# Token-wise attention product in one run, two heads on the two halves of the array's rows; FFN units on three PSUM banks

## The chip, the cores and the metric

One core of one Trainium2 chip. The time is what the device takes for one execution, in microseconds, as a median of several executions. The kernel before takes 315.76 us (315.75 to 315.96 in 3 runs). Engines are named as in the profile: PE (TensorE), PEld (its weight loads), DVE, ACT, POOL, and SP, which here only issues DMAs.

## The reference, cut to what matters

```python
kv  = einsum('bhsd,bhse->bhde', k, v)        # 8 batches, 8 heads, 576 tokens, 64 per head
out = einsum('bhsd,bhde->bhse', q, kv)
rms = sqrt(mean(out * out, axis=-1, keepdims=True) + 1e-6)
x   = (out / rms * g_norm)                   # laid out as (8 * 576 tokens, 512)
y   = ((x @ w_a) * (x @ w_b)) @ w_out        # d_ff = 1536
```

The FFN is the bulk of the work. It runs in 9 strips of 512 tokens. The attention of batch s+1 is worked on during strip s, between the FFN's matmuls. A batch has 576 tokens and a strip 512, so a strip needs only the first part of the newest batch.

## The kernel before

A strip has 12 units (eight matmuls of 512 columns each: `a`, then `b`) and 4 output pieces (12 matmuls each). A slot number `n` counts them, `n + 0.5` is the middle of the next one. For batches 2 to 7, x is made by token: `tx` multiplies a chunk of 128 tokens by the kv matrices of two heads at once, which stand as two 64x64 blocks on the diagonal of a 128x128 matrix `kvb` with zeros elsewhere. The squares, sums and scaling follow on ACT, DVE and POOL, and a transposing DMA on the SP queue brings the chunk into `xt`, from which the FFN's matmuls read.

```python
def tx(self, c, i):                                  # chunk c into bank i
    for p in range(NP):                              # 4 pairs of heads
        nc.tensor.matmul(P[:, i, p * 128 : (p + 1) * 128],
            lhsT=self.qT[:, p, t0 : t0 + 128], rhs=kvb[self.b % 2][:, p, :], start=True, stop=True)
    nc.scalar.activation(sqt[c % 3][r], self.by_head(i)[r], AF.Square)
# tss: DVE sum; trs: ACT reciprocal root, POOL scale; then
def txt(self, c, i):
    nc.vector.tensor_mul(t[r], self.by_head(i)[r], sqt[c % 3][r])
    nc.sync.dma_start_transpose(xt[:, :, ...], ...)  # x transpose, on the SP queue
...
AB = (4, 1, 2, 0)                                    # PSUM banks of the FFN units, in turn
...
if s == 1: k0, xs = 5, (6.5, 8, 9.5, 11, 12.5)       # slots: kv product, chunks 0..4
...                                                  # txt of a chunk: 2.5 slots after its tx
for s in range(1, N_STRIP - 1):
    for n in range(FC + 4):
        ...  ffn_ab or ffn_o (its output store goes to the SP queue), then slot(A, s, n)
        if b + 1 < B and n == (12, 4, 8, 5, 8)[s - 1]:
            transpose_q(b + 1)                       # q load, transposing, on the SP queue
        if b + 2 < B and n == (14, 10, 14, 8)[s - 1]:
            load_late(b + 2)                         # q, k, v of batch b+2, issued by POOL
```

X transposes, output stores and q loads share one queue, and their order on it is the order in which this program issues them.

## Time and profile before

| | before |
|---|---|
| time, median | 315.76 us |
| PE busy | 98% of the span |
| matmul of the FFN, 512 columns | issues every 216 ns |
| token-wise product | 120 matmuls, 56 ns each, 6.7 us |

From the page of the kernel before, the busy shares and the chain that ended last:

```profile
span 313.9 us, 4977 instructions
PE 308.9 (98%) x1907; PEld 147.9 (47%) x1907; DVE 141.6 (45%) x235; ACT 115.9 (37%) x225; POOL 101.2 (32%) x123
...
PE 98%; ACT 1%; issue 0%; DVE 0%
```

PE is the bound: its work makes up 98% of the chain. The longest wait of PE, in the waits view (engine, line, waited for: us in total, times, longest), is one of the start:

```profile
PE P L400 <- DVE eps_t L417: 1.2, 1, 1.2
```

The timeline of PE gives the costs (start, length, engine, source line, instruction, shapes, count). The ends of matmuls are modelled and overlap, so costs are read from starts. First the token-wise product of one chunk, between units:

```profile
64.22 0.39 PE L265 MATMUL P<-kvb,qT 128*128 128x128 bf16 x4
64.44 1.03 PE L315 MATMUL P<-xt,wb_t 128*128 128x512 bf16 x4
```

Four matmuls of the product (L265) move the next group from 64.22 to 64.44 us: 0.22 us, 56 ns each. Then a kv burst, which runs in pairs on the two halves of the array's columns:

```profile
124.29 1.03 PE L315 MATMUL P<-xt,wb_t 128*128 128x512 bf16 x4
125.25 1.46 PE L168 MATMUL P<-vtl,ktl 128*64 128x64 bf16 x80
126.63 1.04 PE L315 MATMUL P<-xt,wa_t 128*128 128x512 bf16 x4
127.51 1.03 PE L315 MATMUL P<-xt,wb_t 128*128 128x512 bf16 x4
```

With 0.863 us for a group of four FFN matmuls, the burst of 80 moves what follows by 127.51 - 0.863 - (124.29 + 0.863) = 1.49 us. The bursts of 40 move it by 0.86 us. So a pair takes about 31.7 ns and a burst about 0.23 us besides.

### The profile page before, as it was taken

How to read it: one execution, taken by the hardware profiler on the slowest of the kernel's cores; microseconds unless marked ns; L12 is line 12 of the kernel's file. 1: busy time of each engine (PE TensorE's matmuls, PEld its weight loads, DVE VectorE, ACT ScalarE, POOL GpSimd, SP SyncE). 2: the span in 40 equal slices, each digit the busy share in tenths (PEclk: the TensorE clock that was granted, in tenths of full speed). 3: DMA queues.
4: the chain of work that ended last, by engine and by line, in shares of the span. 5: the costliest groups of instructions: out<-in, count | busy, mean ns of one | idle time of the engine just before them, and what ended most of it. 6: DMA issues, size and time to landing. Idle time of an engine off the chain costs nothing.

```text
span 313.9 us, 4977 instructions
## 1 busy us (share of the span) xinstructions
PE 308.9 (98%) x1907; PEld 147.9 (47%) x1907; DVE 141.6 (45%) x235; ACT 115.9 (37%) x225; POOL 101.2 (32%) x123
## 2 busy tenths in 40 slices
PE   8999999999999999999999999999999999999995
PEld 3544454444445444544454445544544444444443
DVE  4544335456337703583377123761683134214321
ACT  3643255453246313451364024622651233123310
POOL 8954990282453730148138200320230000000000
PEclk9999999999999999999999999999999999999999
DMA  8999999999899999059999980073022200030002
GB/s 181 196 196 199 201 186 166 230 136 152 165 162 184 103 199 151 2 58 162 212 120 130 158 186 2 19 159 109 3 50 60 102 0 0 33 102 1 0 34 101
DMA packets 94253, 36.19 MB, mean 115 GB/s; under 512 B 64918, under 2 KB 89750, under 8 KB 94230
## 3 DMA queue, kind: packets, MB, share of 16 engines
q0 software_dynamic: 59120, 18.44, 54.3%
q1 hardware_dynamic: 34642, 16.87, 24.7%
q10 hardware_dynamic: 468, 0.57, 0.6%
q8 instruction: 15, 0.25, 0.3%
q14 instruction: 8, 0.07, 0.1%
HBM read 37.78 MB, written 12.98 MB: 162 GB/s over the span
## 4 chain that ended last, share of the span: by engine, by line
PE 98%; ACT 1%; issue 0%; DVE 0%
PE P L315 60%; PE P L372 30%; PE P L265 2%; PE P L400 2%; PE P L168 2%; PE P L192 1%; PE P L219 1%; PE P L206 0%; ACT sq L215 0%; PE P L245 0%; PE P L458 0%; ACT o_end L610 0%; PE P L462 0%; PE P L474 0%; DVE zeros L411 0%
## 5 line engine op out<-in xcount | busy, mean ns | idle before, releaser
L333 DVE TENSOR_TENSOR ab<-P,asb 128x512 bf16<-128x512 f32 x108 | 74.5, 691 | 103.6 <-PE P L315 86.0
L315 PE MATMUL P<-xt,wa_t 128*128 128x512 bf16 x432 | 111.9, 380 | 0.0
L315 PE MATMUL P<-xt,wb_t 128*128 128x512 bf16 x432 | 111.7, 379 | 0.0
L329 ACT CAST asb<-P 128x512 bf16<-128x512 f32 x108 | 63.0, 585 | 92.7 <-PE P L315 92.7
L372 PE MATMUL P<-wo_t,ab 128*128 128x512 bf16 (+1 forms) x444 | 95.8, 374 | 0.0
L372 PEld LDWEIGHTS <-ab 128*128 128x128 bf16 x444 | 43.0, 98 | 48.6
L315 PEld LDWEIGHTS <-wa_t 128*128 128x128 bf16 x432 | 41.4, 98 | 47.4 <-issue 0.2
L315 PEld LDWEIGHTS <-wb_t 128*128 128x128 bf16 x432 | 41.5, 98 | 46.9
L288 POOL TENSOR_TENSOR sqt<-rst,g_all 128x512 f32<-128x512 f32 (+1 forms) x24 | 25.0, 1043 | 96.2 <-ACT rst L281 96.2
L385 ACT COPY osb<-P 128x512 f32<-128x512 f32 x17 | 9.9, 585 | 67.3 <-PE P L372 57.5
L387 DVE COPY osb<-P 128x512 f32<-128x512 f32 x18 | 12.4, 691 | 44.1 <-PE P L372 39.5
L139 POOL DMA_DIRECT2D qs<-in_q_dram x12 | 19.8, 1653 | 0.7 <-issue 0.3
L276 DVE TENSOR_REDUCE sst<-sqt 128x8 f32<-128x512 f32 (+1 forms) x24 | 16.3, 680 | 1.8 <-ACT sqt L272 1.1
L297 DVE TENSOR_TENSOR qv<-P,sqt 128x512 bf16<-128x512 f32 (+1 forms) x24 | 16.4, 685 | 0.3
L272 ACT ACTIVATE sqt<-P 128x512 f32<-128x512 f32 (+1 forms) x24 | 14.4, 599 | 4.2 <-PE P L265 4.1
L265 PEld LDWEIGHTS <-qT 128*128 128x128 bf16 x120 | 9.2, 98 | 7.1
L265 PE MATMUL P<-kvb,qT 128*128 128x128 bf16 x120 | 11.6, 219 | 0.0
L281 ACT ACTIVATE rst<-sst,eps_t 128x8 f32<-128x8 f32 (+1 forms) x30 | 9.0, 300 | 4.6 <-DVE sst L276 4.3
L233 DVE SCALAR_TENSOR_TENSOR xt<-P,g_col,rs 128x288 bf16<-128x288 f32 x16 | 7.5, 512 | 5.2 <-ACT rs L223 5.2
L288 POOL TENSOR_TENSOR k_x<-rst,g_all 128x512 f32<-128x512 f32 x6 | 6.3, 1042 | 8.8 <-ACT rst L281 8.8
L131 POOL DMA_DIRECT2D wo_t<-in_moe_w_out_dram x12 | 6.4, 530 | 6.7 <-DMA wb_t<-in_moe_w_b_dram 3.2
L400 PE MATMUL P<-zeros 128*128 128x512 bf16 x17 | 7.2, 568 | 1.2 <-DVE eps_t L417 1.2
(67 smaller groups left out, 119.4 us busy)
## 6 DMA issues: line engine op xcount, KB each, us to landing
out_dram<-osb SPq DMA_DIRECT2D x23, 256.0 KB, 2.1
qs<-in_q_dram POOLq DMA_DIRECT2D x12, 288.0 KB, 7.0
ktl<-in_k_dram POOLq DMA_DIRECT2D x6, 512.0 KB, 9.2
vtl<-in_v_dram POOLq DMA_DIRECT2D x6, 512.0 KB, 11.9
out_dram<-osb SPq DMA_DIRECT2D x13, 128.0 KB, 2.4
wo_t<-in_moe_w_out_dram POOLq DMA_DIRECT2D x12, 128.0 KB, 6.0
wa_t<-in_moe_w_a_dram POOLq DMA_DIRECT2D x5, 256.0 KB, 9.0
wb_t<-in_moe_w_b_dram POOLq DMA_DIRECT2D x5, 256.0 KB, 9.6
```

The source lines that it names most:

```text
L139: nc.gpsimd.dma_start(out=d[:, hs, :], in_=q[b, hs].rearrange("h t d -> t h d"))
L265: nc.tensor.matmul(P[:, i, p * 128 : (p + 1) * 128], lhsT=self.qT[:, p, t0 : t0 + 128], rhs=kvb[self.b % 2][:, p, :], start=True, stop=True,)
L272: nc.scalar.activation(sqt[c % 3][r], self.by_head(i)[r], AF.Square)
L276: nc.vector.reduce_sum(sst[c % 3][r], sqt[c % 3][r], axis=mybir.AxisListType.X)
L288: nc.gpsimd.tensor_mul(sqt[c % 3][r], rst[c % 3][r].unsqueeze(2).to_broadcast([n, H, D]), g_all[r].unsqueeze(1).to_broadcast([n, H, D]),)
L297: nc.vector.tensor_mul(t[r], self.by_head(i)[r], sqt[c % 3][r])
L315: nc.tensor.matmul(self.a if w is wa_t else self.b, lhsT=w[:, kc, self.fc * 128 : (self.fc + 1) * 128], rhs=xt[:, kc, t0 : t0 + STRIP], st ...
L329: nc.scalar.copy(self.t, self.a)
L333: nc.vector.tensor_mul(abt[self.s % 2][self.fc], self.b, self.t)
L372: nc.tensor.matmul(P[:, i, e0:e1], lhsT=abt[s % 2][fc][:, g * 128 : (g + 1) * 128], rhs=wo_t[:, fc, e0:e1], start=(fc == 0), stop=(fc == F ...
L387: nc.vector.tensor_copy(t, P[:, i, :])
L400: nc.tensor.matmul(P[:, i, 0:cols], lhsT=zeros[:, 0:128], rhs=zeros[:, 0:cols], start=True, stop=True)
```

## The change

Its intent: with the zero blocks gone, two heads can use the upper and the lower 64 rows of the array at the same time, 64 columns each. A change of the array's mode costs something (about 0.2 us a run, as read below), so all of chunks 0 to 3 of a batch are computed in one run, into banks 4 to 7 (the two heads of a pair in different banks). The last, half-used chunk (LC) stays 128 rows wide and goes into bank 3. It is now handled first, so that bank 3 is free for the output pieces. The units are left with banks 0 to 2.

```diff
-        def tx(self, c, i):
+        def tx(self):
             for p in range(NP):
                 nc.tensor.matmul(
-                    P[:, i, p * 128 : (p + 1) * 128],
-                    lhsT=self.qT[:, p, t0 : t0 + 128],
+                    P[:, O, p * 128 : (p + 1) * 128],
+                    lhsT=self.qT[:, p, S - 128 : S],
                     rhs=kvb[self.b % 2][:, p, :],
...
+            for c in range(LC):
+                for p in range(NP):
+                    for j, (i, c0) in enumerate(self.place(c)):   # banks 4..7
+                        r = slice(j * D, (j + 1) * D)
+                        nc.tensor.matmul(
+                            P[:, i, c0 + p * D : c0 + (p + 1) * D],
+                            lhsT=self.qT[r, p, t0 : t0 + 128],
+                            rhs=self.kvs[r, p, :],
...
-    AB = (4, 1, 2, 0)
+    ab_banks = [4, 1, 2, 0]            # later [0, 1, 2]
...
+        k0, x0 = {1: (5, 6.5), 2: (2, 3.5), 3: (5, 6.5), 4: (0, 1.5), 5: (5, 6.5), 6: (0, 1.5)}[s]
...
-                a.kv_out(slice(0, NP), kb[:, i], nc.vector.tensor_copy if i else nc.scalar.copy)
+                nc.vector.tensor_copy(a.kvs, kb[:, i])
+                a.kv_out(slice(0, NP), kb[:, i])
+        if n == x0:
+            A.tx()
+        for i, c in enumerate((LC, *range(LC))):
+            m = n - x0                 # tsq at 1.5 * i; tss at (1, 2, 4, 5, 7)[i];
+            ...                        # trs half a slot, txt 1.5 slots after tss
...
-            if b + 2 < B and n == (14, 10, 14, 8)[s - 1]:
+            if b + 2 < B and n == (14, 11, 14, 9)[s - 1]:
                 load_late(b + 2)
```

More of the change, by code (lines that the diff above doesn't have):

```diff
@@ L78 @@
     k32 = k_x[0:EP].rearrange("p (h c d) -> p h c d", h=2, c=EC)
-    sqt = [sb([128, H, D], FP32, f"sqt{i}") for i in range(2)]
-    sqt.append(k_x[:, 0 : H * D].rearrange("p (h d) -> p h d", h=H))
+    sqt = [sb([128, 2, NP, D], FP32, f"sqt{i}") for i in range(2)]
+    sqt.append(k_x[:, 0 : H * D].rearrange("p (j h d) -> p j h d", j=2, h=NP))
     sst = [sb([128, H], FP32, f"sst{i}") for i in range(3)]
@@ L257, in rows, with place, by_head @@
             return t0, slice(c * 128 - t0, 128)
-        def by_head(self, i):
-            return P[:, i, :].rearrange("t (h d) -> t h d", h=H)
-        def tx(self, c, i):
-            t0, r = self.rows(c)
+        def place(self, c):
+            return tuple((4 + 2 * j + c // 2, c % 2 * (STRIP // 2)) for j in range(2))
+        def by_head(self, c):
+            if c == LC:
+                return P[:, O, :].rearrange("t (p j d) -> t j p d", j=2, p=NP)
+            (i, c0), (j, _) = self.place(c)
+            o = P[:, i : j + 1 : j - i, c0 : c0 + STRIP // 2]
+            return o.rearrange("t j (p d) -> t j p d", p=NP)
+        def tx(self):
             for p in range(NP):
                 nc.tensor.matmul(
-                    P[:, i, p * 128 : (p + 1) * 128],
-                    lhsT=self.qT[:, p, t0 : t0 + 128],
+                    P[:, O, p * 128 : (p + 1) * 128],
+                    lhsT=self.qT[:, p, S - 128 : S],
                     rhs=kvb[self.b % 2][:, p, :],
@@ L271, in tx, with tsq @@
                 )
-            nc.scalar.activation(sqt[c % 3][r], self.by_head(i)[r], AF.Square)
+            for c in range(LC):
+                t0, _ = self.rows(c)
+                for p in range(NP):
[5 more added lines that the diff above has]
+                            rhs=self.kvs[r, p, :],
+                            start=True,
+                            stop=True,
+                        )
+        def tsq(self, c):
+            _, r = self.rows(c)
+            nc.scalar.activation(sqt[(c + 1) % (LC + 1) % 3][r], self.by_head(c)[r], AF.Square)
         def tss(self, c):
             _, r = self.rows(c)
-            nc.vector.reduce_sum(sst[c % 3][r], sqt[c % 3][r], axis=mybir.AxisListType.X)
+            nc.vector.reduce_sum(
+                sst[(c + 1) % (LC + 1) % 3][r],
+                sqt[(c + 1) % (LC + 1) % 3][r].rearrange("t j p d -> t (j p) d"),
+                axis=mybir.AxisListType.X,
+            )
         def trs(self, c):
@@ L281, in trs @@
             nc.scalar.activation(
-                rst[c % 3][r],
-                sst[c % 3][r],
+                rst[(c + 1) % (LC + 1) % 3][r],
+                sst[(c + 1) % (LC + 1) % 3][r],
                 AF.Abs_reciprocal_sqrt,
@@ L288, in trs, with txt @@
             nc.gpsimd.tensor_mul(
-                sqt[c % 3][r],
-                rst[c % 3][r].unsqueeze(2).to_broadcast([n, H, D]),
+                sqt[(c + 1) % (LC + 1) % 3][r].rearrange("t j p d -> t (j p) d"),
+                rst[(c + 1) % (LC + 1) % 3][r].unsqueeze(2).to_broadcast([n, H, D]),
                 g_all[r].unsqueeze(1).to_broadcast([n, H, D]),
             )
-        def txt(self, c, i):
+        def txt(self, c):
             t0, r = self.rows(c)
             t = x_tok[c // 3][:, c % 3]
-            nc.vector.tensor_mul(t[r], self.by_head(i)[r], sqt[c % 3][r])
+            nc.vector.tensor_mul(
+                t[r].rearrange("t (p j) d -> t j p d", j=2), self.by_head(c)[r], sqt[(c + 1) % (LC + 1) % 3][r]
+            )
             t0 += self.b * S
@@ L337, in rest @@
             self.part_b(kcs)
-    AB = (4, 1, 2, 0)
-    n_ab = [0]
+    ab_banks = [4, 1, 2, 0]
     def ab_bank():
-        n_ab[0] += 1
-        return AB[(n_ab[0] - 1) % len(AB)]
+        ab_banks.append(ab_banks.pop(0))
+        return ab_banks[-1]
     def ffn_ab(s, fc, between=None):
@@ L516 @@
     u3.part_b()
-    n_ab[0] = 0
     for fc in range(4, FC):
@@ L550 @@
     u1.rest((3,))
-    n_ab[0] = 1
+    ab_banks[:] = [0, 1, 2]
     def slot(A, s, n):
@@ L568, in slot @@
             for i, a in enumerate(two):
-                a.kv_out(slice(0, NP), kb[:, i], nc.vector.tensor_copy if i else nc.scalar.copy)
-        for c, x in enumerate(xs):
-            i = 5 + c % 3
-            if n == x:
-                A.tx(c, i)
-            elif n == x + 0.5:
+                nc.vector.tensor_copy(a.kvs, kb[:, i])
[4 more added lines that the diff above has]
+            m = n - x0
+            if m == 1.5 * i:
+                A.tsq(c)
+            if m == (1, 2, 4, 5, 7)[i]:
                 A.tss(c)
-            elif n == x + 1:
+            if m == (1, 2, 4, 5, 7)[i] + 0.5:
                 A.trs(c)
-            elif n == x + 2.5:
-                A.txt(c, i)
+            if m == (1, 2, 4, 5, 7)[i] + 1.5:
+                A.txt(c)
     for s in range(1, N_STRIP - 1):
```

## The prediction

> **What bounds the kernel.** TensorE. The page gives PE 98% busy at full granted clock; the chain that ended last is 98% PE and after the start holds no wait worth naming. DVE (45%), ACT (37%), POOL (32%) have room. So only PE's issue time counts, unless PE is made to wait. In the timeline an FFN matmul of 512 columns issues every 216 ns (12 in 2.59 us), a unit of eight takes 1.73 us.
>
> **What changes on PE.** For batches 2 to 7 the token-wise attention product is 20 matmuls of 128x128 (120 in all). The timeline shows four of them moving the next group by 0.22 us: 56 ns each, weight loads hidden; six batches cost 6.7 us. Afterwards the last, half-used chunk stays so (4 matmuls). The 16 others become 32 of 64 rows by 64 columns, in pairs on the two halves of the array's rows, without the zero blocks.
>
> What a pair costs is not in the trace. The nearest thing is the k·v product: pairs on two halves of the *columns*, 64 columns each. A burst of 40 moves the next group by 0.86 us, one of 80 by 1.49 us: 31.7 ns a pair, plus 0.23 us fixed per burst. The Trainium skill says both: "TensorE: Matmul & The Clock Gate", Part 3, that row tiles run concurrently; "TensorEngine Tiling (Array Packing)", Key Properties, that a change of tiling mode drains the array. The trace agrees for column halves; no run shows yet that 64-row by 128-column weight loads keep that pace.
>
> Estimate per batch: before 16 x 56 = 0.89 us; after 16 x 31.7 ns + 0.23 us = 0.73 us. Gain 0.16 us, times six 1.0 us, all of it on the critical path. One run per batch keeps the fixed cost below the gain.
>
> **What changes elsewhere.** Squares, reductions, scalings stay the same in number and size, spread over 8.5 units rather than 7.5. The kv copies add one DVE copy (about 0.4 us) per batch; all half-block copies (about 0.37 us) now go to ACT, four in a row (1.5 us) where two batches are prepared; the product needs them 2.6 us after the kv burst. Not critical.
>
> Three banks instead of four for the units: a bank is written again 1.73 us after its group's issue ends. From the timeline the ACT eviction is done 0.78 us, the DVE multiply 0.97 us after that end: slack 0.95 and 0.76 us. Two 0.68 us DVE jobs between two multiplies fit with about 0.3 us delay, less than the slack. I expect no or only tenths of a microsecond of PE waits.
>
> **Prediction.** 314.8 us (0.3% faster), 8 in 10 between 314.1 and 316.4. Faster by over 2%: 0.01; within 2%: 0.96; slower by over 2%: 0.03.
>
> **What would show it.** Right: the 32 narrow matmuls plus 4 wide ones move the following group by about 0.95 us a batch, against 1.12 us for the 20 before; no idle before FFN matmuls. Three-bank step wrong: FFN matmuls waiting on the asb copy or ab multiply. Pair step wrong: the run takes 1.1 to 1.4 us.
>
> **What would make it wrong.** If the halves run one after another, 32 x 29 ns plus the fixed cost is 1.16 us a batch: 1.6 us slower in all. If weight loads of 64 rows don't hide (no pace under 53 ns a pair), about 1 us slower. If DVE's order makes a multiply wait over 0.8 us for a reduction, each batch could lose 0.5 us. A larger drain for row halves also eats the gain.

## More of the kernel before

Last the SP queue near the end of strip 1.

```profile
76.39 1.11 SPq L365 DMA_DIRECT2D out_dram<-osb  x2
77.60 1.25 SPq L299 DMA_TRANSPOSE xt<-qv  x1
79.02 2.63 SPq L151 DMA_TRANSPOSE qT<-qs  x1
81.75 0.99 SPq L365 DMA_DIRECT2D out_dram<-osb  x2
82.83 1.90 SPq L299 DMA_TRANSPOSE xt<-qv  x1
```

The x transpose at 77.60 us is that of chunk 2, the last one that strip 2 needs. The trace has no time of landing for it (the moment at which a DMA's data are in place), but strip 2 started at 83.47 us without a wait, so it had landed by then. The q load behind it holds SP for 2.63 us.

## The result, and the profile after

The changed kernel takes 320.25 us (319.04 to 320.56 in 5 runs), the kernel before in the same rounds 315.76 us: ratio 1.0135, 95% interval 1.0117 to 1.0154. A ratio is the mean time of one kernel's runs over that of the other's of the same rounds, so not quite the ratio of the medians quoted. Executions over 1.5% slower than the fastest of the same kernel are left out of the means. I had predicted 314.8 us, with a range up to 316.4.

The page of the changed kernel, with the parts shown of before:

```profile
span 318.5 us, 5155 instructions
PE 309.3 (97%) x2003; PEld 146.0 (46%) x2003; DVE 142.3 (45%) x237; ACT 117.5 (37%) x229; POOL 101.0 (32%) x123
...
PE 84%; DMA 8%; POOL 4%; issue 1%; DVE 0%; SPq 0%; ACT 0%; POOLq 0%; DVEq 0%
```

DMAs are now in the chain that ended last. The waits view for PE names them:

```profile
PE P L346 <- DMA xt<-qv: 2.6, 1, 2.6
PE P L430 <- DVE eps_t L447: 1.2, 1, 1.2
PE P L168 <- DMA vtl<-in_v_dram: 1.2, 1, 1.2
```

The middle one is the start of the kernel and stood before, too. There is no FFN matmul (L346, L402) that waits for ACT or DVE: the three banks cost nothing. The two others are new.

The run itself went better than predicted (timeline of PE):

```profile
64.26 0.39 PE L275 MATMUL P<-kvb,qT 128*128 128x128 bf16 x4
64.58 0.64 PE L287 MATMUL P<-kvs,qT 64*128 64x64 bf16 x32
65.15 1.04 PE L346 MATMUL P<-xt,wb_t 128*128 128x512 bf16 x4
66.03 1.03 PE L346 MATMUL P<-xt,wa_t 128*128 128x512 bf16 x4
```

It moves what follows by 66.03 - 0.863 - 64.26 = 0.91 us, where the 20 matmuls of before moved it by 5 x 0.22 = 1.12 us: 0.21 us gained per batch, 1.3 us for six. The starts of the single matmuls in the trace show where the time goes: the two of a pair start 3 to 4 ns apart, and a pair follows every 29 ns. The first narrow matmul starts 0.15 us after the last wide one, and the next FFN matmul 0.12 us after the last narrow one. In `e4_full_rows` below, where the mode does not change, these distances are 0.06 and 0.03 us. So the two changes of mode cost about 0.09 us each.

**First wait, at the start of strip 2.** The SP queue:

```profile
76.44 1.11 SPq L395 DMA_DIRECT2D out_dram<-osb  x2
77.65 1.25 SPq L330 DMA_TRANSPOSE xt<-qv  x1
79.07 2.35 SPq L151 DMA_TRANSPOSE qT<-qs  x1
81.51 0.99 SPq L395 DMA_DIRECT2D out_dram<-osb  x2
82.60 1.85 SPq L330 DMA_TRANSPOSE xt<-qv  x1
```

It looks like the one of before. But the x transpose at 77.65 us is now that of chunk 1, since the last chunk goes first and all others one place later. Chunk 2 is the one at 82.60 us, behind the q load and a store, although DVE had finished it at 78.4 us. It landed at 86.0 us. PE was through with strip 1 at about 83.5 us:

```profile
86.04 1.33 PE L346 MATMUL P<-xt,wa_t 128*128 128x512 bf16 x4 [2.58 <-DMA xt<-qv]
87.16 1.91 PE L346 MATMUL P<-xt,wb_t 128*128 128x512 bf16 x4
88.86 1.61 PE L346 MATMUL P<-xt,wa_t 128*128 128x512 bf16 x4
...
93.00 0.82 PE L168 MATMUL P<-vtl,ktl 128*64 128x64 bf16 x40
```

Not only is there a wait of 2.58 us; the groups after it start 1.1 to 1.7 us apart in place of 0.863. The windows view shows why: its third number from the end is the granted clock.

```profile
84.00:86.00 2.00, 0.00 (x0) 0.00 (x0) 0.00 (x0) 0.08 (x1) 0.80 (x2) 1.00 0.68 118
86.00:88.00 2.00, 1.96 (x6) 0.74 (x6) 0.00 (x0) 0.58 (x1) 2.00 (x2) 0.66 0.80 199
88.00:90.00 2.00, 2.00 (x6) 0.76 (x5) 0.69 (x1) 0.00 (x0) 2.00 (x3) 0.50 1.75 125
```

After the idle stretch PE ran for about 3.4 us at half the clock ((0.34 + 0.50) x 2 us / 0.5). By the chain, the first 24 matmuls of strip 2 took 7.03 us, in the kernel before 5.18 us: 1.85 us more. Not all of this is the clock. By starts the 24 took 93.00 - 86.04 = 6.96 us, and 91.30 - 86.03 = 5.27 us in `e2_q5_later` below, which waited as long but kept its clock: 1.7 us are the clock's. The other 0.16 us belong to the wait, which the profile counts from a modelled end. The Trainium skill, "TensorE: Matmul & The Clock Gate", Part 1, says that the clock halves after an idle window of about 3.4 us which runs freely. This agrees in kind: the clock went to 0.50. But the idle time here was only 2.6 us. And the wait does not always cost the clock: of the five runs of this kernel four have a mean clock of 0.994 or 0.995, but the fastest, at 319.04 us, has 0.999.

**Second wait, in the kv burst of strip 3**, which needs v of batch 5:

```profile
131.02 0.95 PE L168 MATMUL P<-vtl,ktl 128*64 128x64 bf16 x48
133.12 0.69 PE L168 MATMUL P<-vtl,ktl 128*64 128x64 bf16 x32 [1.15 <-DMA vtl<-in_v_dram]
133.74 1.04 PE L346 MATMUL P<-xt,wa_t 128*128 128x512 bf16 x4
```

The burst moves what follows from 131.02 to 133.74, 2.72 us, and before from 125.25 to 126.63, 1.38 us: 1.34 us more. The view of the v tile says how long its two DMAs took from issue to landing, before and then after:

```profile
DMA to landing us min/median/max: 11.8/12.0/12.2
```

```profile
DMA to landing us min/median/max: 13.6/14.4/15.1
```

And SP started the q load of batch 5 in the midst of it (v was issued from 117.1 us on); in the kernel before that load stood behind the first x transpose of batch 4, at 136.97 us:

```profile
121.88 6.33 SPq L151 DMA_TRANSPOSE qT<-qs  x1
```

The sum of these readings, with 6 x 0.213 = 1.28 us for the gain: 2.58 + 1.85 + 1.34 - 1.28 = 4.49 us. The medians differ by 320.25 - 315.76 = 4.49 us.

### The profile page after: what moved, and what is told of

Its sections match the earlier page's. It is cut to its first block, busy times and chain, and to the rows that moved or that the text cites. A ratio compares the mean times of both kernels' runs of the same rounds, so it can differ in the third digit from the quotient of the medians.

```text
span 318.5 us, 5155 instructions
## 1 busy us (share of the span) xinstructions
PE 309.3 (97%) x2003; PEld 146.0 (46%) x2003; DVE 142.3 (45%) x237; ACT 117.5 (37%) x229; POOL 101.0 (32%) x123
## 4 chain that ended last, share of the span: by engine, by line
PE 84%; DMA 8%; POOL 4%; issue 1%; DVE 0%; SPq 0%; ACT 0%; POOLq 0%; DVEq 0%
PE P L346 55%; PE P L402 25%; DMA vtl<-in_v_dram 5%; DMA wb_t<-in_moe_w_b_dram 2%; PE P L168 1%; PE P L287 1%; DMA xt<-qv 1%; POOL qt L116 1%; POOL qs L139 1%; POOL vt L116 1%; PE P L192 0%; POOL wa_t L464 0%; POOL kt L116 0%; PE P L275 0%; PE P L219 0%
## 5 line engine op out<-in xcount | busy, mean ns | idle before, releaser
L364 DVE TENSOR_TENSOR ab<-P,asb 128x512 bf16<-128x512 f32 x108 | 74.4, 691 | 107.5 <-PE P L346 101.0
L346 PE MATMUL P<-xt,wa_t 128*128 128x512 bf16 x432 | 112.8, 382 | 2.6 <-DMA xt<-qv 2.6
L346 PE MATMUL P<-xt,wb_t 128*128 128x512 bf16 x432 | 112.7, 382 | 0.1
L402 PE MATMUL P<-wo_t,ab 128*128 128x512 bf16 (+1 forms) x444 | 95.6, 374 | 0.0
L346 PEld LDWEIGHTS <-wa_t 128*128 128x128 bf16 x432 | 42.1, 98 | 53.3 <-issue 4.2
L402 PEld LDWEIGHTS <-ab 128*128 128x128 bf16 x444 | 43.1, 98 | 49.1
L346 PEld LDWEIGHTS <-wb_t 128*128 128x128 bf16 x432 | 42.0, 98 | 50.9 <-issue 1.2
L417 DVE COPY osb<-P 128x512 f32<-128x512 f32 x18 | 12.5, 692 | 41.0 <-PE P L402 40.9
L179 ACT CAST kvb<-P 64x256 bf16<-64x256 f32 (+1 forms) x20 | 6.0, 301 | 14.6 <-DVE kvs L599 9.5
L223 ACT ACTIVATE rs<-P,eps_t 128x576 f32<-128x576 f32 (+1 forms) x9 | 6.1, 688 | 4.0 <-PE P L219 3.8
L430 PE MATMUL P<-zeros 128*128 128x512 bf16 x17 | 6.2, 503 | 1.2 <-DVE eps_t L447 1.2
## 6 DMA issues: line engine op xcount, KB each, us to landing
vtl<-in_v_dram POOLq DMA_DIRECT2D x6, 512.0 KB, 11.9
```

Of the source, the lines that this page charges most:

```text
L346: nc.tensor.matmul(self.a if w is wa_t else self.b, lhsT=w[:, kc, self.fc * 128 : (self.fc + 1) * 128], rhs=xt[:, kc, t0 : t0 + STRIP], st ...
L364: nc.vector.tensor_mul(abt[self.s % 2][self.fc], self.b, self.t)
L402: nc.tensor.matmul(P[:, i, e0:e1], lhsT=abt[s % 2][fc][:, g * 128 : (g + 1) * 128], rhs=wo_t[:, fc, e0:e1], start=(fc == 0), stop=(fc == F ...
L417: nc.vector.tensor_copy(t, P[:, i, :])
```

## The experiments

My theory after the result: the matmul change is a gain of 1.3 us, and both losses come from the order on the SP queue. The chunks' x transposes moved later in the program, past two q loads that stayed where they were. The first one then stands in front of chunk 2; the second one is no longer held back by an x transpose, and disturbs the v load. Rivals: the three banks or the new DVE order make PE late; v is late because its own issue moved; the gain comes from fewer columns, not from concurrency.

### Remove the cause: q loads one unit later

`e1_q3_later` (q of batch 3), on the changed kernel:

```diff
-            if b + 1 < B and n == (12, 4, 8, 5, 8)[s - 1]:
+            if b + 1 < B and n == (13, 4, 8, 5, 8)[s - 1]:
```

> The changed kernel, with the transposing load of q for batch 3 issued one unit later, behind the x transpose of batch 2's third chunk. Theory (order on the SP queue): in the changed kernel that third chunk is ready at 78.4 us but its transpose is issued at 82.6 us, behind the q load and a store, so strip 2 waits 2.6 us and then runs 1.9 us longer at a lowered clock. Here the wait and the lowered clock go: about 4.4 us less, 315.9 us, span near 314.2 us; the wait for the v load near 131 us stays. Rival (three banks or the longer DVE order make units late): 320.2 us, unchanged.

Measured 316.75 us (316.48 to 316.96; one slow run of 321.9 us at clock 0.989 is left out), ratio to before 1.0026. The wait for x fell from 2.6 to 0.8 us and the clock stayed at 1.00; the wait for v stayed (0.9 us). 3.5 us of the expected 4.4 came back.

`e2_q5_later` (q of batch 5):

```diff
+            if b + 1 < B and n == (12, 4, 9, 5, 8)[s - 1]:
```

> The changed kernel, with the transposing load of q for batch 5 one unit later, behind the first x transpose of batch 4. Theory (that load, no longer held back by an x transpose, runs beside the v load of batch 5 and slows it from 12.2 to 15.1 us): the v load lands in about 12 us, the wait of the k.v product goes, about 1.3 us less: 318.9 us; the wait at strip 2's start stays. Rival (the v load is simply issued too late, because it moved one unit and stands behind a scaling on POOL): v lands after 15 us and the wait of 1.2 us stays, 320.2 us.

Measured 317.38 us (317.21 to 318.33), ratio 1.0052. v landed in 12.0 to 12.4 us though it was still issued behind the same POOL work, and the wait for v is gone. That falsifies the rival for the second wait. It gained 2.9 us, more than expected, and the reason is the clock. The wait for x was 2.7 us as before, but this time no clock was lost. The windows view of this run, right after its wait:

```profile
86.00:88.00 2.00, 1.97 (x10) 0.90 (x10) 0.00 (x0) 0.59 (x1) 2.00 (x2) 1.00 0.81 202
88.00:90.00 2.00, 2.00 (x11) 0.93 (x10) 0.94 (x2) 0.59 (x1) 2.00 (x3) 1.00 1.71 121
```

So an idle time of 2.6 or 2.7 us may or may not lower the clock. What decides it is not shown by these runs. If the window runs freely, as the skill's page has it, it can matter where in it the idle time falls; no run tested this, and a whole window of 3.4 us without work does not fit into 2.6 us.

`e3_both_later` (both):

```diff
+            if b + 1 < B and n == (13, 4, 9, 5, 8)[s - 1]:
```

> Both q loads one unit later. Theory: both waits go, and the gain on PE shows: 20 matmuls of 56 ns per batch became a run of 0.90 us, 0.21 us less, times six 1.3 us: 314.5 us, faster than the kernel before by 0.4%. Rival (banks or DVE order cost something too): no faster than 315.8 us, with PE waits on the asb copy or the ab multiply.

Measured 315.78 us (315.15 to 316.31), ratio 0.9994, interval 0.9981 to 1.0007. In the profiled run, which at 315.15 us was the fastest, the losses are gone except for 0.7 us: no wait on ACT or DVE in the strips, none for v, but PE still waits 0.7 us for x. The other runs, up to 1.2 us longer, have no profile. Chunk 2's transpose is issued at 79.9 us here (77.6 before) and lands 4.0 us later. The expected 314.5 was missed because I had forgotten that the new order finishes chunk 2 on DVE 1.5 us later than before, too.

### Is it concurrency?

`e4_full_rows`, on `e3_both_later`: the same 32 narrow matmuls, but each over all 128 rows, with the zero blocks.

```diff
-                            lhsT=self.qT[r, p, t0 : t0 + 128],
-                            rhs=self.kvs[r, p, :],
+                            lhsT=self.qT[:, p, t0 : t0 + 128],
+                            rhs=kvb[self.b % 2][:, p, r],
```

> As the run with both q loads later, but the 32 narrow matmuls per batch use all 128 rows with the zero blocks (one head's 64 columns each), so they can't run side by side. Everything else is the same. If pairs run together, as the 0.57 us run suggests: here 32 x 29 ns = 0.93 us in place of 0.68 with its mode changes, 0.25 us more per batch, 1.5 us in all: 316.0 us. Rival (the halves aren't really concurrent, the gain comes from the smaller column count alone): within 0.3 us of 314.5 us.

Measured 317.16 us (316.82 to 317.83), ratio 1.0044: 1.4 us slower than `e3_both_later` by the medians, of which at most 0.3 us are the wait for x (1.0 here, 0.7 there). The run itself, in the timeline of PE:

```profile
64.13 0.39 PE L275 MATMUL P<-kvb,qT 128*128 128x128 bf16 x4
64.36 1.10 PE L287 MATMUL P<-kvb,qT 128*128 128x64 bf16 x32
65.29 0.81 PE L346 MATMUL P<-xt,wb_t 128*128 128x512 bf16 x3
```

The 32 take 65.29 - 64.36 = 0.93 us, 29 ns each, one after the other, and there is no mode change. On the row halves the whole step was 0.91 us with the wide four, here it is 65.29 - 64.13 = 1.16 us. So the halves do run side by side; narrow columns alone would have made the change slower than before, not faster.

### Put the cause into the kernel before

These runs change nothing on PE. The first two were too weak, and tell something by that.

`e5_before_q3_early`:

```diff
-            if b + 1 < B and n == (12, 4, 8, 5, 8)[s - 1]:
+            if b + 1 < B and n == (11, 4, 8, 5, 8)[s - 1]:
```

> The kernel BEFORE with one number changed: the q load of batch 3 issued one unit earlier, so that it stands ahead of the x transpose of batch 2's third chunk, as it does in the changed kernel. No matmul, bank or DVE order changes. Theory (order on the SP queue is the cause of the wait at strip 2): the third chunk's transpose is issued near 82.6 us in place of 77.6, PE waits about 2.6 us at strip 2's start; with the clock kept 318.5 us, with it lowered for some microseconds up to 320.3 us. Rival (the new chunk order on DVE, the pairs or the banks are needed for the loss): 315.9 us, unchanged.

Measured 315.82 us, ratio 0.9999: no wait. The q load went out at 74.45 us into a gap in which SP had nothing else to do. Chunk 2's transpose followed at 80.20 us and came in time. My expectation had wrongly assumed that this q load waits for its data until 79 us. In fact it had only been waiting for its turn; what costs is the time for which it holds SP (2.3 to 2.4 us in the runs where it delays chunk 2).

`e9_before_x_order` repeats it with the right dose: chunk 1's transpose is issued at slot 12 and chunk 2's at slot 13, so that the order on SP is that of the changed kernel.

```diff
+            if self.b == 2 and c in (1, 2):
+                return                       # txt: DVE work only
+            self.send(c)                     # send: the dma_start_transpose
...
+            if s == 1 and n in (12, 13):
+                A.send(n - 11)
```

> The kernel BEFORE in which only two x transposes of batch 2 (second and third chunk) are issued later on the SP queue, one on each side of the q load and of the store, in the same order as in the changed kernel. Matmuls, banks and the work of DVE, ACT and POOL stay. The earlier run with the q load one unit earlier was too weak a dose: it filled an idle gap of SP, and the third chunk's transpose still went out at 80.2 us. Theory (the order on SP alone causes the wait at strip 2): here it goes out near 82.6 us, PE waits about 2.6 us at strip 2's start: 318.5 us if the clock is kept, up to 320.3 us if it is lowered. Rival (the pairs or the banks are needed): 315.9 us.

Measured 317.78 us (317.59 to 317.86), ratio 1.0063, interval 1.0048 to 1.0078. The waits view of PE:

```profile
PE P L323 <- DMA xt<-qv: 1.6, 1, 1.6
```

Chunk 2's transpose went out at 82.72 us, and the kernel before, otherwise untouched, became 2.0 us slower. The wait is shorter than the 2.6 us expected: x was there at 85.47 us (86.04 in the changed kernel), and strip 1 ended some 0.4 us later here. The clock was kept. So the order on SP alone makes the first wait; neither row halves nor banks are needed.

For the second wait, `e6_before_q5_early` puts the q load of batch 5 ahead of the first x transpose of batch 4:

```diff
+            if b + 1 < B and n == (12, 4, 7, 5, 8)[s - 1]:
```

> The kernel BEFORE with one number changed: the q load of batch 5 one unit earlier, ahead of the first x transpose of batch 4. Theory (that load then starts near 118 us beside the v load of batch 5 and slows it): v lands after about 15 us in place of 12.2, the k.v product waits 0.5 to 1.2 us: about 316.7 us. Rival (v was late in the changed kernel because its issue moved): no wait, 315.9 us.

Measured 315.79 us, ratio 0.9998: no wait. v took 12.6 to 13.1 us. I then suspected that the load of v has to be issued one unit later as well, and ran that alone (`e10_before_load_late`) and with the early q load (`e11_before_load_late_q5_early`):

```diff
-            if b + 2 < B and n == (14, 10, 14, 8)[s - 1]:
+            if b + 2 < B and n == (14, 11, 14, 8)[s - 1]:
```

> The kernel BEFORE with the loads of batch 5 issued one unit later, as in the changed kernel, but the k.v product left where it is. This is the control for the next run. From the kernel before: v issued near 113.6 us, lands 12.2 us later, near 125.8 us, about when the second half of the k.v product asks for it: no wait or some tenths, 315.9 to 316.4 us.

> As the control, and with the q load of batch 5 one unit earlier, so that it starts about 4 us after the v load's issue, as in the changed kernel (in the run with the q load alone it started 5.9 us after, and v took only 12.8 to 13.1 us). Theory (the q load beside the v load slows it): v lands after 14 to 15 us and PE waits 2 to 3 us more than in the control: 318 to 319 us. Rival: as the control.

Measured 315.69 us (ratio 0.9998) and 315.76 us (0.9999). The edit did not do what it was meant to do. The loads already stood behind POOL's last scaling of that batch, and the built programs turned out to have the same instructions in the same order on every engine: the control is the kernel before once more, and the other run is `e6_before_q5_early` once more. As such they show the spread: v took 12.1 to 12.5 us (before: 11.8 to 12.2) without the early q load, and 12.6 to 13.1 and 13.7 to 14.1 us with it. But in `e5_before_q3_early`, where no q load runs beside it, v took 12.6 to 13.1 us, too. So the q load slows v here by 2 us at most, and `e6_before_q5_early` alone does not show that it slows it. No time was lost, as v comes about 2 us before it is asked for (in the kernel before issued at 111.8 us, landed 12.2 us later at the latest; the second half of the burst starts at about 125.25 + 0.75 = 126.0 us). In `e11_before_load_late_q5_early` it landed at 126.0 us, just in time.

`e12_in_order_q5_early` makes the test on the fastest version below, by one number:

```diff
-            if b + 1 < B and n == (12, 4, 9, 5, 8)[s - 1]:
+            if b + 1 < B and n == (12, 4, 8, 5, 8)[s - 1]:
```

> The fastest version so far with only the q load of batch 5 back at its old place (ahead of the first x transpose of batch 4). Theory: v lands after about 15 us again and PE waits 1.0 to 1.3 us in the k.v product: 315.5 to 315.9 us against 314.5 us. Rival (the wait needs strip 2's delay as well): 314.5 us.

Measured 316.43 us (315.95 to 319.04; the run of 319.04 had a clock of 0.995), ratio 1.0038, interval 0.9997 to 1.0080, against 0.9956 for the version without it. Tile view of v and waits view of PE:

```profile
DMA to landing us min/median/max: 15.8/16.0/16.1
```

```profile
PE P L168 <- DMA vtl<-in_v_dram: 2.0, 2, 1.1
```

The wait is longer than the 1.0 to 1.3 us expected, as v took 16 us, not 15. Strip 2 starts without a wait here, so the second loss needs no help from the first. In this run the q load started at 117.45 us, 4.1 us after the last v DMA was issued (113.40); in the kernel before with the early q load the distance was 5.9 to 6.0 us and the effect smaller. v is issued later in the changed kernels because POOL's last scaling is (107.5 us here, 105.9 us before), while the stores in front of the q load end at about the same time. That the distance sets the size of the effect fits these numbers, but no run varied it alone.

### The banks, alone

`e7_before_3banks`, on the kernel before:

```diff
-    AB = (4, 1, 2, 0)
+    AB = (2, 1, 0)
```

> The kernel BEFORE with the units on three banks (2, 1, 0) in place of four. Theory (a bank's eviction is done 0.8 to 1.0 us after its group's issue ends, 1.73 us are there): no waits, within 0.3 us of 315.9 us. Rival (the third bank's loss explains the part of the PE gain that is still missing with both q loads later): 0.5 to 1 us slower, with FFN matmuls waiting on the asb copy or the ab multiply.

Measured 315.76 us (315.43 to 315.90) against 315.90, ratio 0.9995, interval 0.9983 to 1.0008, with no PE wait on ACT or DVE in the units. Three banks are enough.

### A version that beats both

`e8_strip1_in_order`: for batch 2 only, chunks 0 to 3 go before the last one, so chunk 2 is again ahead of the q load. The last chunk then holds bank 3 during the output pieces of strip 1, and these take the units' banks, which are free then.

```diff
-        for i, c in enumerate((LC, *range(LC))):
+        for i, c in enumerate((*range(LC), LC) if s == 1 else (LC, *range(LC))):
...
-                ffn_o(s, n - FC, ab_bank() if n % 2 else O, amid)
+                ffn_o(s, n - FC, ab_bank() if n % 2 or s == 1 else O, amid)
...
-            if b + 1 < B and n == (12, 4, 8, 5, 8)[s - 1]:
+            if b + 1 < B and n == (12, 4, 9, 5, 8)[s - 1]:
```

> The changed kernel with chunks 0 to 3 ahead of the last one for batch 2 only (its output stage then keeps off the bank that the last chunk holds), the q load of batch 3 back at its old place, that of batch 5 one unit later. Theory (with both q loads later, 0.7 us of wait for the third chunk's transpose were left, since its DVE work and so its issue come 2.4 us later than before, at 79.9 us): issued near 77.5 us as before, no wait at all, so the whole PE gain of 1.3 us shows: 314.6 us, ratio 0.996, faster than both kernels. Rival (something else eats the gain): within 0.3 us of 315.8 us.

Measured 314.54 us (314.27 to 314.58) against 315.90, ratio 0.9956, interval 0.9942 to 0.9969: faster than both. The waits of PE and the SP queue:

```profile
PE P L430 <- DVE eps_t L447: 1.2, 1, 1.2
PE P L219 <- ACT sq L215: 0.4, 1, 0.4
```

```profile
77.70 1.25 SPq L330 DMA_TRANSPOSE xt<-qv  x1
79.12 2.51 SPq L151 DMA_TRANSPOSE qT<-qs  x1
...
82.81 1.81 SPq L330 DMA_TRANSPOSE xt<-qv  x1
```

The queue has the same form and nearly the same times as in the changed kernel. Only which chunk stands at 77.70 us is different, and that is worth a wait. The waits that are left are those of the start.

## Why the prediction was wrong

- **PE is the bound, and the row halves run side by side: right.** Costs were a little too high. I took the rate of the column halves, 0.73 us for the 32 with the mode change, and 0.95 us for the whole run; it took 0.91 us. The gain is 0.21 us per batch, 1.3 us in all, where I had said 1.0 us. The fastest version, at 1.36 us under the kernel before, shows this gain with nothing else in the way. Two places of the Trainium skill stood behind the step: "TensorE: Matmul & The Clock Gate", Part 3, for row tiles that run concurrently, and "TensorEngine Tiling (Array Packing)", Key Properties, for the drain at a mode change. `e4_full_rows` agrees with the first, 0.25 us per batch. The trace agrees with the second: about 0.09 us for each change of mode, and a pair of row halves every 29 ns where I had taken 31.7.
- **Three banks: right.** The estimated slacks of 0.95 and 0.76 us held; `e7_before_3banks` costs nothing, and the changed kernel has no wait on ACT or DVE.
- **"What changes elsewhere ... Not critical", and "no or only tenths of a microsecond of PE waits": this failed.** I asked only whether ACT, DVE and the banks would keep PE waiting. I wrote myself that the chain of a batch is "spread over 8.5 units rather than 7.5", and did not go on to ask what waits at its end. At its end stand the x transposes on the SP queue, and the q loads there had kept their slots. So chunk 2 fell behind a q load (2.58 us of wait and 1.85 us after it, of which 1.7 us are the lowered clock), and the other q load came loose and ran beside the v load (1.34 us). The first wait follows from the order on SP alone (1.6 us in `e9_before_x_order`, where the clock was kept). The second needs more than that order: in the kernel before it cost nothing (`e6_before_q5_early`, ratio 0.9998). The list of what would make the prediction wrong has no DMA in it.
- **The range.** 316.4 us as the upper end is 0.6 us above the kernel before. That left room for a late multiply in one batch (0.5 us), but not even for the serial halves (1.6 us) of the prediction's own list. Neither came to pass. A wait long enough to cost the clock as well was not in it.

What stays open: when an idle time of 2.6 us lowers the clock and when it does not; why the same q load costs v less in the kernel before; and what exactly makes the q load slow the v load down (the runs show only that it does: 11.9 to 12.4 us without it in `e2_q5_later` and `e8_strip1_in_order`, 13.6 to 16.1 us with it in the changed kernel and `e12_in_order_q5_early`).

## What to carry to other kernels

When a change moves the end of a chain later, list what leaves it by DMA, and compare the queue's order before and after by what each entry carries, not by its form: the same five lines on SP were harmless with chunk 2 in second place and cost up to 4.4 us, the lowered clock included, with chunk 1 there. An entry that seems late because of its data may only have been waiting for its turn, and one that is early enough today may be so only because something stands in front of it. A PE that is 98% busy has no room for a wait: 2.6 us idle cost up to 1.7 us more by the clock.

## What the Trainium skill lacked or had wrong

- "DMA: Bandwidth & Descriptors", Issuing engines are not separate DMA queues: it calls the time to initiate a DMA on the sequencer "usually small relative to the DMA itself". Here an x transpose held SP for 1.2 us or more and landed 2.3 to 4.3 us after issue in most cases, and a q load held it for 2.1 to 7.4 us and landed after 4.4 to 12.7 us; that was enough to cause the first wait.
- No page that I found says by how much a DMA transpose from DRAM slows a load issued by POOL that is under way: 12.3 us to landing became 16.1 us (`e8_strip1_in_order` and `e12_in_order_q5_early`).
- "TensorE: Matmul & The Clock Gate", Part 1, gives an idle window of about 3.4 us before the clock halves. Here 2.6 us were followed by a clock of 0.50 in one kernel, and 2.7 us by none in another; in the changed kernel itself, one run of five kept its clock (0.999).
- The same page, Part 2, Back-to-back issue gap, gives a sustained 81 ns for matmuls of 128 columns with their weight loads and 131 ns for 512 columns. Here they issue every 56 and 216 ns in a full stream; the formula which the page calls that of an isolated gap fits better. (Under "Step-by-step", the same Part has these 56 and 216 ns for back-to-back matmuls, so that it contradicts itself.)
- The same page, Part 3, has no rate for pairs with 64 columns and a weight load each, and no page that I found has the time of a mode change: here a pair took 29 ns and a change of mode about 0.09 us.
